# A list of units on one core: routing steps moved to the head of VectorE's list, and four smaller moves

## The chip, the core and the metric

The kernel runs on one core of a Trainium2 chip. Five engines work side by side on their own instruction lists: TensorE (PE, matrix products and transposes into PSUM), VectorE (DVE), ScalarE (ACT), GpSimd (POOL, which also issues the indirect transfers) and SyncE (SP, which issues the plain loads). An engine works through its list in order; an instruction that waits holds everything behind it on that engine. The metric is the device time of one execution in microseconds, taken as the median of several runs.

## What is computed

The reference is an mLSTM cell over 4 batches, 8 heads, 768 steps and a head width of 40, whose rows then go through a mixture of experts with top-1 routing in two levels (4 groups of 4 experts):

```python
m_new = max(f + m, i);  f_stab = exp(f + m - m_new);  i_stab = exp(i - m_new)
C = f_stab * C + i_stab * outer(v, k);   n = f_stab * n + i_stab * k
y = sigmoid(o) * (C @ q) / max(|n . q|, 1)          # x: 3072 rows of 320
g = argmax(x @ w_group);  e = argmax(x @ w_expert[g])  # one of 16 experts
out = softmax_g * softmax_e * (relu(x @ w1[g, e]) @ w2[g, e])
```

## The kernel before

The cell is computed in chunks of 128 steps: 6 chunks times 4 batches make 24 units, numbered u = 0 to 23, one after the other. The function `unit(u)` writes the instructions of one step of this pipeline, and since the schedule is manual there, each engine's list is in the order in which `unit` calls things. In unit u TensorE does, in this order: `scores(u)` (key times query, 16 products into `sp`), `turn(u - 2)` (three transposes of the finished rows `x` into the bank `av`, which ScalarE copies to `xT`), `state(u)` (update of the running sums `Cp`), a few transposes of the gate sums (`sum_on`), `back(u - 1)` (four transposes of the unit before into `av`, after ScalarE's copy of `xT` has freed that bank), `carried(u)` (the part of the result that comes from earlier chunks, into `avT`), in some units the routing products, and `values(u)` (the part from this chunk, into `avT`, which needs VectorE's masked scores `pt` and GpSimd's scaled values `vz`). VectorE does `masked` (two products, `pt`), `norm(u - 1)` and `rows(u - 1)` (`den` and `xn`). GpSimd does `rows2(u - 1)` (`x` from `xn` and `den`) and `vscale(u + 1)` (`vz`). ScalarE turns the gate, copies `Cp` to `Cs` (`state2`) and `avT` to `avs`.

Routing goes by groups of units, `GROUPS` = (0 to 3), (4 to 7), (8 to 11), (12 to 15), (16, 17), (18 to 21), (22, 23). After a group's rows are turned, `logits_of` makes its logits in the bank `lg`, and the generator `route` is appended to `chores`. Each `go_on(n)` runs its next n steps. The steps are: 1 maxima, differences (and an Exp on ScalarE); 2 `eq`; 3 `m2` and the one-hot rows of the levels; 4 `oh`; 5 the ranks, small products of `oh` on TensorE (L343 to L352); 6 and 7 slots and counts; 8 to 11 the weight of each row; 12 the slots are put on the list `ids`; 13 and 14 the running count. The tables `FIRST`, `RANKS`, `MID` and `END` say how many steps run at which place of which unit. An entry of `ids` is written by `put_id`, one indirect transfer by GpSimd (L448), one or two at the end of a unit and all that are left before unit 21. After the last of them SyncE reads the index list `ix` of the first expert, GpSimd gathers its rows `xg` (L543), and TensorE turns them in unit 23 (`turn_tasks`, into the banks `Cp`), ahead of `values(23)`. Expert 0 follows, then the others.

The weights of the first expert come during units 12 to 19. They are split into two parts by `split_tasks`: ScalarE casts a piece to fp32r (L607), and VectorE subtracts it from the original in the next unit (`lows`, L609). The gates' running maxima and sums are made by the generators `gate_sums`, of which `sum_on` runs a step or two in each unit; their transposes went into the free half of the bank `avT_125` (`AV[1]`).

Of the kernel before, what the change touches and what calls it, by code (L numbers as in the profile page):

```python
# [18 lines left out]
P = 128  # L19
B, H, S, D = 4, 8, 768, 40  # L20
NCH = S // P
NU = NCH * B
# [34 lines left out]
def bc(ap, shape):  # L57
    return ap.broadcast_to(list(shape))
# [3 lines left out]
def lstm_moe(ctx: ExitStack, tc: tile.TileContext, gates, qkT, nat, wcat, w1, w2, cst, seq, out):  # L62
    nc = tc.nc
# [56 lines left out]
    AV = [ps_a.tile([P, 512], F32, name=f"avT{i}") for i in range(2)]  # L120
# [5 lines left out]
    def busy(n):  # L126
        if n:
            t = ps_1.tile([P, 512], F32, name="busy", tag="lg")
        for _ in range(n):
            mm(t, ones_b, bc(ones_b.unsqueeze(1), (P, 4, P)), start=True, stop=True)  # L130
# [23 lines left out]
    def gate_o(u):  # L154
        o = st_[u]["nt"][:, 2 * DM:3 * DM]
        nc.scalar.activation(o, o, AF.Tanh, scale=0.5)
# [27 lines left out]
    def masked(u, r):  # L184
        t = st_[u]
        pt = wk.tile([P, 4, P], F32, name="pt", bufs=4)
        nc.vector.tensor_tensor(pt, t["pm"][r], bc(cs[:, C_UP:C_UP + P].unsqueeze(1), (P, 4, P)), op=ALU.mult)  # L187
        t["pm"][r] = pt
# [66 lines left out]

    def rows2(u):
        x = tail.tile([P, 3 * P], F32, name="x", bufs=NU - EUNITS)
        (nc.gpsimd if u < NU - 2 else nc.vector).tensor_tensor(  # L258
            x[:, 0:DM].rearrange("p (h d) -> p h d", d=D), st_[u]["xn"], bc(st_[u]["den"].unsqueeze(2), (P, H, D)), op=ALU.mult)
        st_[u]["x"] = x  # L260

# [22 lines left out]
    def bank_of(tag):  # L284
        return (pools["t"] if tag == "tp" else ps_1).tile([P, 512], F32, name=tag)
# [5 lines left out]
    def logits_of(u0, u1):  # L291

        n = u1 - u0
        bank = bank_of("lg")
        t = bank[:, P:2 * P]
        for k in range(3):
            for b in range(n):
                mm(t[32 * b:32 * b + 32, :], wc[:, k, :], st_[u0 + b]["xT"][:, k, :], start=(k == 0), stop=(k == 2))
        lT = wk.tile([P, P], F32, name="lT", bufs=1)
        nc.scalar.copy(lT[0:32 * n], t[0:32 * n])  # L300

        def back():
            nc.tensor.transpose(out=bank[:, 0:32 * n], in_=lT[0:32 * n], identity=ident[0:32 * n, 0:32 * n])
            chores.append(route(u0, u1, bank))

        backs.append(back)
# [91 lines left out]
    def go_on(n=1):  # L398
        for _ in range(n):
            if chores:  # L400
                with ExitStack() as st:
                    if not rt["manual"]:
                        st.enter_context(tc.high_priority())
                    if next(chores[0], StopIteration) is StopIteration:
                        chores.pop(0)
# [32 lines left out]
    def first_tokens():  # L438
        none, zero = rt["rows"]
        nc.sync.dma_start(itab[0:4 * P].rearrange("(p a) e w -> p (a e) w", p=P), none)  # L440
        nc.sync.dma_start(itab[NTOK], none[0:NE, 0, :])
        nc.sync.dma_start(x_d[0:1], zero[0:1])
# [338 lines left out]
    def run(stage, u):  # L781
        if 0 <= u < NU:
            stage(u)

    def do(tasks, n=99):
        while tasks and n:
            tasks.pop(0)()
            n -= 1

    def ix_of(r):  # L790
        return lambda i, m, w: ixs[r][0:m, i, w:w + 1]

    xgs, early_loads, early_splits = {}, [], []

    def unit(u):
        run(loads, u + 3)
        if u == 6:
            first_tokens()
        run(scores, u)
        go_on(FIRST.get(u, 0))  # L800
        run(lambda v: masked(v, 0), u)
        run(lambda v: masked(v, 1), u)
        run(turn, u - 2)
        if u == 0:
            busy(5)
        run(state, u)
        if u < 13:
            sum_on(SUMS.get(u, 1))
        run(back, u - 1)
        run(norm, u - 1)  # L810
        run(rows, u - 1)
        if u < B:
            run(rows2, u - 1)
        if u < NU - 2:
            run(vscale, u + 1)
        if u == NU - 3:
            run(vscale, u + 2)
        if u >= B:
            run(rows2, u - 1)
        do(lows)  # L820
        run(carried, u)
        go_on(RANKS.get(u, 0))
        if u % B == 1 and 1 < u < EUNITS:
            logits_of(u - 5, u - 1)
        if u == EUNITS + 1:
            logits_of(EUNITS - 2, EUNITS)
        if u == NU - 1:
            logits_of(EUNITS, NU - 2)
        if u == 11:
            go_on(2)  # L830
            chores.insert(0, first_experts())
        if u == EUNITS + 3:
            chores.append(early_counts())
        go_on(MID.get(u, 0))
        if u == NU - 1:
            do(rt["turns"])
        gate_o(u)
        run(state2, u)
        run(values, u)
        do(backs)  # L840
        go_on(END.get(u, 0))
        if u == 3:
            first_entries()
        if u == 5:
            first_rows()
        for _ in range(min(rt.get("old", 0), 1 if u < 16 else 2)):
            put_id()
        rt["old"] = len(ids)

    SUMS = {1: 2}  # L850
    FIRST = {19: 2, 20: 4}
    RANKS = {20: 1}
    MID = {6: 4, 7: 2, 8: 3, 9: 4, 10: 4, 11: 5, 12: 6, 13: 8, 14: 6, 15: 2, 16: 4, 17: 3, 18: 4, 19: 7, 20: 8, 21: 4, 22: 4}
    END = {6: 1, 10: 1, 14: 1, 18: 1}

    def gate_sums(lo, hi):
        fg, ig = G[:, 0, lo:hi], G[:, 1, lo:hi]
        q = nc.gpsimd if lo == 0 else nc.vector
        init = NEG if lo == 0 else M_[:, lo - 1:lo]
        nc.vector.tensor_tensor_scan(M_[:, lo:hi], fg, ig, init, op0=ALU.add, op1=ALU.max)  # L860
        l1 = max(lo, 1)
        q.tensor_tensor(Cg[:, lo:hi], ig, M_[:, lo:hi], op=ALU.subtract)
        yield
        nc.vector.tensor_tensor(Dl[:, l1:hi], G[:, 0, l1:hi], M_[:, l1 - 1:hi - 1], op=ALU.add)
        nc.vector.tensor_tensor(Dl[:, l1:hi], Dl[:, l1:hi], M_[:, l1:hi], op=ALU.subtract)
        yield
        nc.vector.tensor_tensor_scan(A_[:, lo:hi], Dl[:, lo:hi], low[:, lo:hi], 0.0 if lo == 0 else A_[:, lo - 1:lo],
                                     op0=ALU.add, op1=ALU.max)
        q.tensor_tensor(Cg[:, lo:hi], Cg[:, lo:hi], A_[:, lo:hi], op=ALU.subtract)
        yield  # L870
        cl, ch = lo // P, hi // P
        tp = AV[1][:, 2 * P:]
        n = ch - cl
        for i in range(n):
            s = slice((cl + i) * P, (cl + i + 1) * P)
            nc.tensor.transpose(out=tp[:, 32 * i:32 * i + 32], in_=Cg[:, s], identity=ident[0:32, 0:32])
            nc.tensor.transpose(out=tp[:, 32 * (n + i):32 * (n + i) + 32], in_=A_[:, s], identity=ident[0:32, 0:32])
        nc.scalar.activation(eb[:, cl:ch, :].rearrange("p c h -> p (c h)"), tp[:, 0:32 * n], AF.Exp)
        fl = floor[:, cl:ch, :].rearrange("p c h -> p (c h)")
        nc.scalar.activation(fl, tp[:, 32 * n:64 * n], AF.Exp, scale=-1.0)  # L880
        nc.vector.tensor_scalar(fl, fl, 2.0, None, op0=ALU.mult)
        if hi == S:
            yield
            over = post.tile([P, 1], BF16, name="over")[0:B * H]
            nc.vector.tensor_scalar(over, A_[:, S - 1:S], -RANGE, None, op0=ALU.is_le)
            yield
            tp = AV[1][:, 2 * P:]
            mm(tp[:, 0:1], ones_b[0:B * H], over, start=True, stop=True)
            nc.vector.tensor_scalar(wide, tp[:, 0:1], 1.0, None, op0=ALU.min)

# [2 lines left out]
    def sum_on(n=1):  # L893
        for _ in range(n):
            if sums and next(sums[0], StopIteration) is StopIteration:
                sums.pop(0)
# [49 lines left out]
    with tc.manual_schedule():  # L946
        for u in range(5, NU):
            if u == NU - 1:
                rt["turns"] = turn_tasks((0, 0), EARLY, xgs[0], Cp)
            if u == NU - 3:  # L950
                while ids:
                    put_id()
                load_ix(0)
            unit(u)
            do(early_loads, {12: 2, 13: 2, 15: 1, 16: 1, 17: 1, 18: 1, 20: 1, 21: 2, 22: 1, 23: 4}.get(u, 0))
            do(early_splits, {16: 1, 17: 1, 18: 1, 20: 1, 22: 1}.get(u, 0))
            if u == NU - 3:
                xgs[0] = load_x(EARLY, ix_of(0), True)
        go_on(4)
# [313 lines left out]
```

## Time and profile before

| | |
|---|---|
| median of 3 runs | 404.81 us (399.73 to 408.77) |
| the profiled execution | 399.82 us, span 398.2 us, mean granted TensorE clock 0.949 |
| busy | PE 366.3 us (92%), DVE 247.9 (62%), ACT 187.4 (47%), POOL 140.8 (35%) |
| transfers | 82.23 MB, mean 207 GB/s |

The span falls into two parts: the units, up to about 148 us, and the experts behind them. Busy shares are means over both, so each has to be read by itself. A number in square brackets behind a row of the time line is the time that the engine stood idle before it, and who ended that.

### The profile page before, as it was taken

What the parts mean: (1) busy time and instruction counts of PE and PEld (TensorE: products, weight loads), DVE (VectorE), ACT (ScalarE), POOL (GpSimd) and SP (SyncE); (2) the same over time, 40 slices, a digit from 0 to 9 for tenths busy, and PEclk for the clock granted to TensorE, in tenths of its full rate; (3) what the DMA queues carried; (4) which work ended last, traced back from release to release, by engine and by line L of the source; (5) the groups of instructions that cost most, each with busy time, mean ns of one, the idle gap of its engine ahead of it and who ended that gap; (6) DMA issues with size and microseconds to landing.
All of it is one profiled execution on the core that took longest, in us unless ns stands there. A gap on an engine that the chain in (4) does not pass through costs nothing.

```text
span 398.2 us, 9447 instructions
## 1 busy us (share of the span) xinstructions
PE 366.3 (92%) x3572; PEld 328.8 (83%) x3572; DVE 247.9 (62%) x636; ACT 187.4 (47%) x459; POOL 140.8 (35%) x199
## 2 busy tenths in 40 slices
PE   8898997979786698979999999999999999999993
PEld 3676775757665578979999999999999999999993
DVE  5767777856778267574799585576574725553520
ACT  2453434324533233264686555575574725545520
POOL 1264234526656504445223526315123313322210
PEclk9999999979979569987999999999999999999998
DMA  7878677586761620195608978586544567678500
GB/s 197 245 243 258 191 237 244 167 293 219 237 222 48 238 104 31 30 337 201 239 32 311 410 281 280 182 298 237 185 166 161 178 250 247 239 286 307 197 19 15
DMA packets 27383, 82.23 MB, mean 207 GB/s; under 512 B 8800, under 2 KB 12339, under 8 KB 23746
## 3 DMA queue, kind: packets, MB, share of 16 engines
q1 hardware_dynamic: 18946, 63.21, 46.8%
q0 software_dynamic: 4560, 13.16, 9.7%
q10 hardware_dynamic: 3824, 5.18, 3.8%
q8 instruction: 30, 0.49, 0.5%
q14 instruction: 23, 0.19, 0.2%
HBM read 72.70 MB, written 9.10 MB: 205 GB/s over the span
## 4 chain that ended last, share of the span: by engine, by line
PE 72%; DVE 11%; issue 8%; POOL 4%; ACT 3%; POOLq 1%; ACTq 0%; DVEq 0%
PE psh L714 14%; PE psh L682 7%; PE po L737 6%; PE po L738 6%; PE po L736 6%; PE sp L182 5%; PE avT L231 3%; PE av L239 3%; PE po L742 2%; PE av L264 2%; PE avT L222 2%; PE po L741 2%; POOL itab L448 2%; ACT xT L278 1%; PE tp L264 1%
## 5 line engine op out<-in xcount | busy, mean ns | idle before, releaser
L547 POOL DMA_INDIRECT out_dram<-y,ix x32 | 38.3, 1196 | 72.5 <-ACT y L748 57.7
L736 PE MATMUL po<-w2h,hh 128*128 128x320 f32 (+3 forms) x200 | 63.6, 318 | 0.0
L737 PE MATMUL po<-w2l,hh 128*128 128x320 f32 (+3 forms) x200 | 62.4, 312 | 0.0
L738 PE MATMUL po<-w2h,hh 128*128 128x320 f32 (+3 forms) x200 | 62.4, 312 | 0.0
L543 POOL DMA_INDIRECT xg<-x_d,ix x32 | 33.4, 1043 | 72.5 <-DMA ix<-itab 46.8
L609 DVE TENSOR_TENSOR w2l<-w2s,w2h 128x640 fp32r<-128x640 f32 x64 | 50.4, 817 | 12.0 <-ACT w2h L607 11.9
L671 DVE SCALAR_TENSOR_TENSOR hh<-psh,hh 128x240 fp32r<-128x240 f32 (+6 forms) x108 | 36.3, 366 | 21.0 <-ACT hh L668 20.6
L187 DVE TENSOR_TENSOR pt<-sp,cs 128x512 f32<-128x512 f32 x48 | 30.9, 684 | 22.0 <-PE sp L182 22.0
L668 ACT ACTIVATE hh<-psh 128x288 fp32r<-128x288 f32 (+8 forms) x68 | 30.2, 444 | 30.5 <-PE psh L714 15.9
L607 ACT CAST w2h<-w2s 128x640 fp32r<-128x640 f32 x64 | 43.2, 721 | 0.0
L682 PE MATMUL psh<-xhl,w1s 128*128 128x144 f32 (+3 forms) x336 | 41.3, 283 | 0.0
L682 PEld LDWEIGHTS psh<-xhl,w1s 128*128 128x128 f32 x336 | 40.9, 191 | 0.0
L258 POOL TENSOR_TENSOR x<-xn,den 128x320 f32<-128x320 f32 x22 | 18.8, 852 | 55.0 <-DVE xn L253 51.8
L714 PE MATMUL psh<-xhl,w1h 128*128 128x256 f32 (+5 forms) x224 | 37.1, 287 | 0.0
L736 PEld LDWEIGHTS po<-w2h,hh 128*128 128x128 f32 (+3 forms) x200 | 36.5, 183 | 0.0
L737 PEld LDWEIGHTS po<-w2l,hh 128*128 128x128 f32 (+3 forms) x200 | 36.5, 183 | 0.0
L738 PEld LDWEIGHTS po<-w2h,hh 128*128 128x128 f32 (+3 forms) x200 | 36.4, 182 | 0.0
L748 ACT ACTIVATE y<-po,ix 128x320 f32<-128x320 f32 (+3 forms) x24 | 12.7, 528 | 47.9 <-PE po L738 43.9
L448 POOL DMA_INDIRECT itab<-ent,slot x24 | 24.3, 1012 | 23.3 <-DVE ent L395 18.8
L714 PEld LDWEIGHTS psh<-xhl,w1h 128*128 128x128 f32 x224 | 31.2, 189 | 0.4 <-PE psh L714 0.2
L182 PE MATMUL sp<-qk 40*128 40x128 f32 x384 | 31.4, 303 | 0.0
L182 PEld LDWEIGHTS sp<-qk 40*128 40x128 f32 x384 | 26.2, 203 | 4.1 <-issue 3.0
(215 smaller groups left out, 717.8 us busy)
## 6 DMA issues: line engine op xcount, KB each, us to landing
w1s<-in_w_dram SPq DMA_DIRECT2D x13, 1536.0 KB
w2s<-in_w_dram SPq DMA_DIRECT2D x13, 1280.0 KB
nt<-in_nat_dram SPq DMA_DIRECT2D x24, 480.0 KB
qk<-in_qkT_dram SPq DMA_DIRECT2D x48, 160.0 KB
x_d<-x ACTq DMA_DIRECT2D x24, 192.0 KB
w1s<-in_w_dram SPq DMA_DIRECT2D x8, 384.0 KB
w2s<-in_w_dram SPq DMA_DIRECT2D x8, 320.0 KB
w1s<-in_w_dram POOLq DMA_DIRECT2D x1, 1536.0 KB, 10.1
```

Of the source, the lines that this page charges most:

```text
L182: mm(t["pm"][r][:, pr, :], qk[rs, 0, pr, :], qk[rs, 1, pr, :], start=True, stop=True)
L448: no_order("ids", nc.gpsimd.indirect_dma_start(out=itab_flat, out_offset=bass.IndirectOffsetOnAxis(ap=sl, axis=0), in_=tk, in_offset=None))
L543: return nc.gpsimd.indirect_dma_start(out=o, out_offset=None, in_=src, in_offset=bass.IndirectOffsetOnAxis(ap=idx, axis=0))
L547: return nc.gpsimd.indirect_dma_start(out=out, out_offset=bass.IndirectOffsetOnAxis(ap=idx, axis=0), in_=y, in_offset=None, bounds_check=N ...
L607: nc.scalar.copy(a, src[:, s])
L609: lows.append(lambda: nc.vector.tensor_tensor(o[rows], src[rows, s], a[rows].bitcast(F32), op=ALU.subtract))
L671: nc.vector.scalar_tensor_tensor(hh[:, f:f + per, dst], src[:, :, t], 0.0, hr.bitcast(F32)[:, :, t], op0=ALU.max, op1=ALU.subtract)
L682: ins = mm(ps[:, g * W:(g + 1) * W], w1s[:, s], xhl[:, k, :], start=(k == 0), stop=(k == 2))
L714: ins = mm(ps[:, g * W:(g + 1) * W], w[:, s], x, start=(n == 0), stop=(n == len(todo) - 1))
L736: mm(po[0:m], hh[:, f, t], w2h[:, s], start=st0, stop=False)
L737: mm(po[0:m], hh[:, f, t], w2l[:, s], start=False, stop=False)
L738: ins = mm(po[0:m], hh[:, f, tl], w2h[:, s], start=False, stop=sp0)
```

## The change

Five things move; the arithmetic is the same. First, the routing steps 1 to 4 of the groups that end with units 3, 7, 11 and 15 run at the head of units 6, 10, 14 and 18, in VectorE's list ahead of `masked`, and their rank products run in the middle of the unit instead of at its end. (The group (16, 17) stood like this already, in unit 20.) Later steps move to earlier units by a few places. Second, `carried(u)` goes from behind `back` to directly behind `turn`. Third, the cast of a weight piece goes from the end of the unit to a place ahead of `state2`, and so ahead of the copies of `avT`. Fourth, `rows2` of units 20 and 21 is done by VectorE instead of GpSimd. Fifth, the gate sums end one unit earlier and their transposes use the bank `lg`.

```diff
-        (nc.gpsimd if u < NU - 2 else nc.vector).tensor_tensor(
+        (nc.gpsimd if u < 20 else nc.vector).tensor_tensor(
...
         run(turn, u - 2)
...
+        run(carried, u)
         run(state, u)
-        if u < 13:
+        if u < 12:
             sum_on(SUMS.get(u, 1))
...
         do(lows)
-        run(carried, u)
         go_on(RANKS.get(u, 0))
...
-        if u == 11:
+        if u == 10:
             go_on(2)
             chores.insert(0, first_experts())
...
         gate_o(u)
+        do(early_splits, SPLITS.get(u, 0))
         run(state2, u)
         run(values, u)
         do(backs)
-        go_on(END.get(u, 0))
...
-    SUMS = {1: 2}
-    FIRST = {19: 2, 20: 4}
-    RANKS = {20: 1}
-    END = {6: 1, 10: 1, 14: 1, 18: 1}
+    SUMS = {1: 2, 4: 2}
+    FIRST = {6: 4, 10: 4, 14: 4, 18: 4, 20: 4}
+    RANKS = {6: 1, 10: 1, 14: 1, 18: 1, 20: 1}
+    SPLITS = {16: 1, 17: 1, 18: 1, 20: 1, 22: 1}
...
-        tp = AV[1][:, 2 * P:]
+        tp = bank_of("lg")
```

VectorE's list around unit 6, before (`pt` of unit 6 is the first row, `mx` to `oh` are steps 1 to 4 of the group (0 to 3)):

```order
L187 TENSOR_TENSOR pt<-sp,cs 128x512 x2
L881 TENSOR_SCALAR floor<-floor 128x64
L246 TENSOR_TENSOR den<-av,floor 128x8
L247 SCALAR_TENSOR_TENSOR den<-av,den 128x8
L248 RECIPROCAL den<-den 128x8
L253 SCALAR_TENSOR_TENSOR xn<-nt,av 128x320
L320 TENSOR_REDUCE mx<-lg 128x20
L322 TENSOR_TENSOR df<-lg,mx 128x80
L330 SCALAR_TENSOR_TENSOR eq<-df,cs 128x80
L333 TENSOR_REDUCE m_706<-eq 128x20
L334 TENSOR_TENSOR oh_702<-eq,m_706 128x80
L338 TENSOR_TENSOR oh<-oh_702 128x64
```

The same place after (`pt` is that of unit 6, `L860` and `L862` are a step of the gate sums):

```order
L320 TENSOR_REDUCE mx<-lg 128x20
L322 TENSOR_TENSOR df<-lg,mx 128x80
L330 SCALAR_TENSOR_TENSOR eq<-df,cs 128x80
L333 TENSOR_REDUCE m_666<-eq 128x20
L334 TENSOR_TENSOR oh_662<-eq,m_666 128x80
L338 TENSOR_TENSOR oh<-oh_662 128x64
L187 TENSOR_TENSOR pt<-sp,cs 128x512 x2
L860 SCALAR_TENSOR_TENSOR w1s<-w1s 32x256
L862 TENSOR_TENSOR w1s<-w1s 32x256
L246 TENSOR_TENSOR den<-av,floor 128x8
L247 SCALAR_TENSOR_TENSOR den<-av,den 128x8
L248 RECIPROCAL den<-den 128x8
```

The six routing instructions went from behind `xn` to a place ahead of the masks.

TensorE's list from unit 6's rank products on, before (`lg<-ohsum` is the last rank product, at the unit's end; then scores, turn, state, back and carried of unit 7, of whose eight rows two are shown):

```order
L347 MATMUL lg<-ohsum_85,ones_66 128x64
L182 MATMUL sp<-qk_103 128x128 x8
L264 MATMUL av<-cs,x 128x128 x3
L204 MATMUL Cp_123<-vz_105,nt 40x41 x8
L239 MATMUL av<-cs,avs 128x128 x4
L222 MATMUL avT_124<-qk_103,Cs 41x128
L222 MATMUL avT_125<-qk_103,Cs 41x128
```

The same place after (`avT<-pt,vz` is `values`, of unit 6 in the second and third row):

```order
L347 MATMUL lg<-ohsum_85,ones_66 128x64
L231 MATMUL avT_124<-pt,vz_104 41x128 x4
L231 MATMUL avT_125<-pt,vz_104 41x128 x4
L182 MATMUL sp<-qk_103 128x128 x8
L264 MATMUL av<-cs,x 128x128 x3
L222 MATMUL avT_124<-qk_103,Cs 41x128
L222 MATMUL avT_125<-qk_103,Cs 41x128
```

The ranks went ahead of `values(6)`, and `carried(7)` ahead of `state(7)` and `back(6)`.

GpSimd's list before, from the last write of `ids` ahead of the first expert's gather (`vz` of units 22 and 23, `x` of unit 20, the gathers, `x` of unit 21):

```order
L447 MEMSET sep 1x1
L448 DMA itab<-ent_72,slot 49168x4
L171 TENSOR_TENSOR vz_105<-nt,eb 128x8x40
L171 TENSOR_TENSOR vz_106<-nt,eb 128x8x40
L258 TENSOR_TENSOR x<-xn,den 128x320
L543 DMA xg<-x_d,ix 128x384 x2
L258 TENSOR_TENSOR x<-xn,den 128x320
```

After:

```order
L447 MEMSET sep 1x1
L448 DMA itab<-ent_72,slot 49168x4
L171 TENSOR_TENSOR vz_105<-nt,eb 128x8x40
L171 TENSOR_TENSOR vz_106<-nt,eb 128x8x40
L543 DMA xg<-x_d,ix 128x384 x2
```

Both `x` left GpSimd's list; each now stands in VectorE's directly behind its `xn`.

## Rows read from the trace of the kernel before

**Rows 1.** Busy time by stretch: PE, PEld, DVE, ACT, POOL, granted clock, DMA share.

```profile
40.55:44.93 4.38, 4.25 (x73) 3.29 (x72) 3.08 (x9) 1.56 (x5) 0.00 (x0) 1.00 0.43 145
34.32:101.36 67.04, 59.23 (x960) 45.79 (x959) 48.84 (x149) 27.20 (x96) 27.18 (x43) 0.95 0.74 231
84.03:91.25 7.22, 7.22 (x74) 5.53 (x72) 2.94 (x9) 1.61 (x5) 1.42 (x3) 0.53 0.72 234
101.62:121.30 19.68, 16.24 (x223) 12.54 (x221) 14.63 (x44) 7.60 (x24) 9.70 (x13) 0.83 0.65 210
125.79:145.82 20.03, 13.81 (x127) 10.04 (x125) 8.21 (x24) 4.22 (x12) 8.21 (x14) 0.57 0.48 166
186.00:370.00 184.00, 183.95 (x1367) 179.79 (x1365) 115.78 (x244) 106.11 (x215) 60.85 (x60) 1.00 0.66 239
```

**Rows 2.** Time line of TensorE: the rank products, one plain unit, two late waits.

```profile
40.30 0.19 PE L343 MATMUL lg<-oh,lt_b 128*128 128x64 bf16 x1 [1.37 <-DVE oh L338]
...
40.55 1.16 PE L182 MATMUL sp<-qk 40*128 40x128 f32 x16
41.65 0.55 PE L264 MATMUL av<-cs,x 128*128 128x128 f32 x3
...
43.92 1.07 PE L231 MATMUL avT<-pt,vz 128*41 128x128 f32 x16
...
61.04 0.19 PE L343 MATMUL lg<-oh,lt_b 128*128 128x64 bf16 x1 [1.69 <-DVE oh L338]
...
83.78 0.19 PE L343 MATMUL lg<-oh,lt_b 128*128 128x64 bf16 x1 [2.66 <-DVE oh L338]
...
132.04 0.90 PE L264 MATMUL av<-cs,x 128*128 128x128 f32 x3 [5.08 <-POOL x L258]
...
144.43 1.46 PE L264 MATMUL Cp<-cs,xg 128*128 128x128 f32 x6
```

**Rows 3.** What TensorE waited for, 0 to 150 us: sum, times, longest.

```profile
PE av L239 <- ACT xT L278: 3.4, 6, 1.1
PE avT L222 <- DVE wide L889: 0.7, 1, 0.7
```

**Rows 4.** Time line of VectorE: unit 6's masks, routing steps 1 to 4.

```profile
35.51 1.29 DVE L187 TENSOR_TENSOR pt<-sp,cs 128x512 f32<-128x512 f32 x2 [2.19 <-PE sp L182]
...
38.32 0.23 DVE L320 TENSOR_REDUCE mx<-lg 128x20 f32<-128x80 f32 x1
...
40.02 0.23 DVE L338 TENSOR_TENSOR oh<-oh 128x64 bf16<-128x64 f32 x1
```

**Rows 5.** Time line of GpSimd: `x` of unit 19, writes, `vz`, second gather.

```profile
121.38 0.72 POOL L258 TENSOR_TENSOR x<-xn,den 128x320 f32<-128x320 f32 x1 [2.21 <-DVE xn L253]
...
126.12 1.24 POOL L448 DMA_INDIRECT itab<-ent,slot  x1 [0.23 <-issue]
...
128.93 0.96 POOL L448 DMA_INDIRECT itab<-ent,slot  x1 [0.21 <-issue]
129.91 1.40 POOL L171 TENSOR_TENSOR vz<-nt,eb 128x320 f32<-128x320 f32 x2
...
135.19 0.95 POOL L543 DMA_INDIRECT xg<-x_d,ix  x1 [0.30 <-issue]
```

**Rows 6.** Time line of ScalarE in unit 16.

```profile
94.78 0.29 ACT L210 COPY Cs<-Cp 104x164 f32<-104x164 f32 x1 [0.91 <-PE avT L222]
95.30 0.81 ACT L233 COPY avs<-avT 128x256 f32<-128x256 f32 x2 [0.23 <-PE avT L231]
96.01 1.05 ACT L607 CAST w1h<-w1s 128x1024 fp32r<-128x1024 f32 x1
```

**Rows 7.** Time line of VectorE: a subtract of unit 21, `x` in unit 23.

```profile
125.70 0.82 DVE L609 TENSOR_TENSOR w2l<-w2s,w2h 128x640 fp32r<-128x640 f32 x1
...
143.15 0.49 DVE L258 TENSOR_TENSOR x<-xn,den 128x320 f32<-128x320 f32 x1
```

**Rows 8.** The two gathers `xg` of 133 to 140 us, issue to landing.

```profile
DMA to landing us min/median/max: 6.3/6.3/6.3
```

More of the change, by code (lines that the diff above doesn't have):

```diff
@@ L848, in unit @@
         rt["old"] = len(ids)
-    SUMS = {1: 2}
-    FIRST = {19: 2, 20: 4}
-    RANKS = {20: 1}
-    MID = {6: 4, 7: 2, 8: 3, 9: 4, 10: 4, 11: 5, 12: 6, 13: 8, 14: 6, 15: 2, 16: 4, 17: 3, 18: 4, 19: 7, 20: 8, 21: 4, 22: 4}
-    END = {6: 1, 10: 1, 14: 1, 18: 1}
+    SUMS = {1: 2, 4: 2}
+    FIRST = {6: 4, 10: 4, 14: 4, 18: 4, 20: 4}
+    RANKS = {6: 1, 10: 1, 14: 1, 18: 1, 20: 1}
+    MID = {6: 2, 7: 3, 8: 4, 10: 3, 11: 5, 12: 6, 13: 7, 14: 2, 15: 3, 16: 2, 17: 2, 18: 3, 19: 6, 20: 8, 21: 4, 22: 1}
+    SPLITS = {16: 1, 17: 1, 18: 1, 20: 1, 22: 1}
     def gate_sums(lo, hi):
@@ L886, in gate_sums @@
             yield
-            tp = AV[1][:, 2 * P:]
+            tp = bank_of("lg")
             mm(tp[:, 0:1], ones_b[0:B * H], over, start=True, stop=True)
@@ L955, in lstm_moe @@
             do(early_loads, {12: 2, 13: 2, 15: 1, 16: 1, 17: 1, 18: 1, 20: 1, 21: 2, 22: 1, 23: 4}.get(u, 0))
-            do(early_splits, {16: 1, 17: 1, 18: 1, 20: 1, 22: 1}.get(u, 0))
             if u == NU - 3:
```

## The prediction

> **What bounds the kernel now.** I read the busy time by stretch first, since the shares of the whole span mix two programs. Between 186 and 370 us TensorE is busy 183.95 of 184.00 us at full clock [rows 1]: the experts are bound by TensorE, nothing in them is touched, and whatever the units save moves that whole block forward and comes out at the end. So the question is only what the units cost, up to about 148 us.
>
> There a plain unit is bound by TensorE too: unit 7 takes 4.38 us with 4.25 busy and VectorE at 3.08 [rows 1]. But twelve units (6 to 17) take 67.04 us, where 12 times 4.38 is 52.6; the time line of TensorE shows where the rest goes [rows 2]. At the end of units 6, 10 and 14 the rank products wait 1.37, 1.69 and 2.66 us for the routing's `oh`, since VectorE does the routing steps last in the unit. After the 2.66 us the clock falls: unit 15 takes 7.22 us at a granted clock of 0.53 [rows 1], that is 2.84 us more than 4.38; after the shorter two it stayed at full. The same wait stands at the end of unit 18, with a slow unit behind it. In unit 22 TensorE waits 5.08 us for `x` of unit 20, which stands behind the writes of `ids` on GpSimd, and from there to 145.82 us the clock is 0.57 in the mean [rows 1, 2]. Besides, `back` waits 3.4 us in six places for the copy `xT`, and unit 12 0.7 us for `wide` [rows 3].
>
> **The change, part by part.**
>
> Routing steps at the head of the unit. Steps 1 to 4 last from 38.32 to 40.25, 1.93 us [rows 4]. VectorE stood idle 2.19 us ahead of unit 6's masks, so most of this falls into time that was empty; the logits are back in `lg` when scores begin. At worst the masks come 1.93 us later. TensorE has 2.27 us of work between the end of scores and `values` (41.65 to 43.92 [rows 2]), which hides that, so I put the new wait at 0 in units 6 and 10. Before unit 14, VectorE has about 1 us of its own list left over (unit 13 carries seven routing steps), so I leave 1.2 us of wait there, my estimate between 0 and 1.93. Gain: 1.37 + 1.69 + (2.66 - 1.2) = 4.5 us, and with a wait under the 1.69 that the clock survived, unit 15 keeps it: 2.84 more. Bounds: the masks' wait is 0 to 1.93 in each of the three.
>
> Gate sums in `lg`, one step earlier: the wait of 0.7 for `wide` goes, because `carried` no longer shares a bank with it. The second step in unit 4 makes a row late there and another in unit 7; I take 0.45 us against it (0 to one `x`, 0.72 [rows 5]).
>
> `carried` behind `turn`. It gives the copy of `xT` another 0.6 us before `back` needs the bank. Outside units 18 to 23, which are costed below, that leaves small change: the two short waits in units 16 and 17 and the 0.13 us between 4.25 busy and 4.38 in each plain unit [rows 1, 3]. I take 0.9 us for twelve units (0 to 2.2). Its price is that it now waits for ScalarE's copies of `avT` earlier: 1.65 us after `values` (scores and turn, 40.55 to 42.20 [rows 2]) instead of behind `back`. In the trace those copies end 0.5 to 0.6 us after `values`: hidden.
>
> Casts ahead of `state2`. A cast is 1.05 us; ScalarE idled 0.91 us before `state2` and 0.23 before the copies in unit 16 [rows 6], 1.14 together. The three casts of `w1` fit, just, so I cost them at 0; what they cost if that cover goes is the slower rival below.
>
> Units 6 to 17 together: 4.5 + 2.84 + 0.7 - 0.45 + 0.9 = 8.5 us.
>
> Units 18 to 20. Here VectorE becomes the bound. From 101.62 to 121.30, where `xn` of unit 19 ends, it was busy 14.63 of 19.68 us [rows 1]; the list is the same, reordered, and with some 0.9 us of waits left in it `xn` comes 4.1 us earlier. The wait in unit 18, the slow unit 19 and a wait for `xT` lie inside this and are not counted again. I expect TensorE to wait about 2 us for the masks in unit 20; it costs nothing beyond this.
>
> Units 21 to 23. With `x` of units 20 and 21 on VectorE (0.49 us each [rows 7]) the wait of 5.08 us goes. What is late next? First `vz` of unit 22, still behind the six writes: they end at 129.89 and it is there at 130.6 [rows 5]. Then the gathered rows: the second gather is issued at 135.19 and lands 6.3 us later, at 141.5 [rows 5, 8]. TensorE turned them at 144.43 [rows 2], so this chain (`xn` of unit 19, `x`, six writes, index list, gathers) had only 2.9 us of slack. Nothing in the change shortens it: it starts 4.1 us earlier with `xn`, and TensorE will stand before the turns for some 5 to 6 us. So of the 5.08 us and of the slow stretch behind it only 2.9 us come out.
>
> That new wait is as long as the one that goes, and the clock fell after that one. I charge a slow unit's price, 2.84 us, behind the turns; the bounds are 0 (it holds) and half of the 13.81 us that TensorE was busy at 0.57 [rows 1], 6.9.
>
> On the chain of writes a rule speaks against the fourth move. In the trace a write took 1.24 us, not 0.96, while VectorE did a subtract of 0.82 us [rows 5, 7]. The Trainium skill, page "GPSIMD Engine Reference", section "1. Specifications", says that GpSimd shares its SBUF interfaces with VectorE and contends with VectorE instructions that have two SBUF inputs; `x` on VectorE is such an instruction. By the rule its whole 0.49 us would be added to the chain, by the row 0.28/0.82 of it, 0.17; the sum would be 0.5 or 0.2 us less of a gain, and I leave both out.
>
> **Sum:** 8.5 + 4.1 + 2.9 - 2.84 = 12.7 us. The profiled execution took 399.82 us, so 387.1. It is the fast end of the runs: the median is 5.0 us above it, by which the sum would be 392. I forecast 388, nearer the profiled one, since waits of the kind that the change removes are a likely source of the spread.
>
> **The rivals.**
>
> The clock holds, or falls earlier and is back by the turns, and unit 14 does not wait: 12.7 + 2.84 + 1.2 = 16.7, 383 us. For it: the clock may fall during the long wait's idle time and recover on the turns. Against: it did not after the 5.08. Chance 0.12.
>
> The wait changes its place: the masks come later than TensorE's 2.27 us of cover in every routing unit, because VectorE enters the unit late. Then units 6, 10 and 14 wait 1.93 each (4.6 us less than I count) and unit 15 is slow again (2.84), and units 18 to 20 gain some 2 us less: 12.7 - 9.4 = 3.3, 396.5 us. For it: VectorE has 48.84 us of work in those 67.04, and less time will be left. Against: the 2.19 us idle ahead of unit 6's masks. Chance 0.13.
>
> The loads become the bound. In units 6 to 17 the DMA engines are busy 0.74 of 67.04 us [rows 1], 49.6 us; squeezed into 58.5 us that is 0.85. If they can do no more than 0.74, the 8.5 us are lost: 395.6 us. Against: SyncE's loads stand three units ahead. Chance 0.10.
>
> Slower: ScalarE's casts hold TensorE at `carried`. If ScalarE comes to a cast no earlier than the end of `values`, cast and copies take 1.05 + 0.81 = 1.86 us [rows 6], more than the 1.65 after which `carried` wants the bank, and `state` and `back` stand behind it on TensorE. That decides: once ScalarE has lost more than the 1.14 us of idle time, each of the five casts goes onto the path, with the copies queued behind it. The price is 4 to 5 us of casts and, if the clock falls each time, 5 times 2.84, together some 19 us against 12.7: 406 us. For it: the fit in unit 16 is 0.1 us. Against: a late copy shows up whole only where ScalarE was already late, and a wait of 0.2 us did not lower the clock anywhere in the trace. Chance 0.05.
>
> **How the numbers follow.** The forecast has 0.60. The low end takes in the first rival and 4 us of luck in the smaller bounds: 379. The high end is the sum on the median's basis, 392, with the masks waiting or the loads late: 399. About 2% (8 us) is what a measurement of this kernel can tell from no change; the line lies at 396.7. Of the second and third rival about half falls on each side of it: faster 0.60 + 0.12 + 0.10 = 0.82, taken as 0.80; slower 0.05; the rest 0.15.
>
> **What the profile after would show.** Right: no wait of TensorE for `oh` at the end of units 6, 10, 14 and 18; full clock from unit 6 to unit 19; unit 18's scores some 8 to 9 us earlier than 101.36; no wait for `x` in unit 22, a short one for `vz`, and a long one, 4 to 7 us, ahead of the turns of `xg`, with a low clock behind it. Wrong: `values` waiting for `pt` by 2 us in several units, `carried` waiting for `avs`, loads that hold `vz`, or turns that start without a wait (then something in units 21 to 23 took the time). The forecast fails by the most if the clock falls in units where I count on it.

## The result and the profile after

The changed kernel takes **384.04 us** (median of 4 runs, 382.14 to 384.81) against 405.35 us of the kernel before (4 runs beside it, 399.73 to 408.77): a ratio of 0.954 with a 95% interval of 0.942 to 0.966, so it is faster. Some executions of the kernel before run at a lower clock, and the ratio is formed from the fast executions of each kernel, so it is not 384.04/405.35. The forecast was 388.0 us with a range of 379 to 399.

The profiled execution took 384.81 us with a span of 383.2 us, against 399.82 and 398.2. All 15.0 us lie ahead of the experts: their first product starts at 133.00 us and not at 148.00. A table by stretch, with the starts of scores(6), of scores(18) and of the first expert product (`psh`) as its borders, shows where they came from:

| us | units 0 to 5 | units 6 to 17 | scores(18) to turns of `xg` | turns to first expert |
|---|---|---|---|---|
| before | 34.32 | 67.04 | 43.07 | 3.57 |
| after | 36.07 | 55.96 | 36.02 | 4.95 |
| saved | -1.75 | 11.08 | 7.05 | -1.38 |

The first view of the changed kernel is the busy time by stretch, with the columns of [rows 1]:

```profile
64.11:68.29 4.18, 4.18 (x73) 3.29 (x72) 3.30 (x12) 2.24 (x8) 2.49 (x4) 1.00 0.65 213
36.07:92.03 55.96, 54.54 (x956) 43.02 (x956) 45.69 (x146) 28.26 (x92) 26.59 (x43) 1.00 0.83 254
78.45:82.63 4.18, 4.18 (x73) 3.29 (x72) 2.84 (x10) 2.24 (x8) 2.51 (x4) 1.00 0.94 312
92.03:108.23 16.20, 13.51 (x224) 10.81 (x223) 14.37 (x47) 8.78 (x28) 10.60 (x14) 0.99 0.85 273
107.24:115.04 7.80, 7.80 (x74) 5.89 (x72) 5.33 (x24) 2.68 (x9) 5.73 (x11) 0.56 0.62 185
128.05:133.00 4.95, 4.64 (x30) 3.27 (x31) 1.84 (x5) 2.33 (x7) 0.00 (x0) 0.63 0.12 45
```

Units 6 to 17 now have TensorE busy for 54.54 of 55.96 us at full clock; before, it was 59.23 of 67.04 [rows 1]. A plain unit (64.11) has no gap left: 4.18 of 4.18, where 4.25 of 4.38 stood. Unit 15, 7.22 us at 0.53 before, takes 4.18 at full clock. From scores(18) to `xn` of unit 19 (92.03 to 108.23) VectorE is busy 14.37 of 16.20 us, so the list that bounds this part has little left in it. Behind unit 6 two slow stretches remain, at 107.24 and behind the turns.

The time line of TensorE of the changed kernel, at the places of [rows 2]:

```profile
17.03 0.55 PE L264 MATMUL av<-cs,x 128*128 128x128 f32 x3 [1.25 <-POOL x L258]
...
18.96 1.86 PE L231 MATMUL avT<-pt,vz 128*41 128x128 f32 x16
...
39.15 0.19 PE L343 MATMUL lg<-oh,lt_b 128*128 128x64 bf16 x1
...
58.46 0.19 PE L343 MATMUL lg<-oh,lt_b 128*128 128x64 bf16 x1
...
77.19 0.19 PE L343 MATMUL lg<-oh,lt_b 128*128 128x64 bf16 x1
...
106.49 0.66 PE L239 MATMUL av<-cs,avs 128*128 128x128 f32 x4 [2.04 <-ACT xT L278]
...
128.05 0.90 PE L264 MATMUL Cp<-cs,xg 128*128 128x128 f32 x3 [5.32 <-DMA xg<-x_d,ix]
129.16 0.90 PE L264 MATMUL Cp<-cs,xg 128*128 128x128 f32 x3 [0.20 <-DMA xg<-x_d,ix]
```

The rank products (L343) of units 6, 10 and 14 carry no wait. What is left is a wait for `x` in unit 2 with a slow product behind it, a wait for `xT` in unit 20, and one of 5.32 us for the gathered rows ahead of the turns, which took the place of the 5.08 us for `x` in unit 22 [rows 2].

The wait for `xT` is explained by ScalarE's time line there:

```profile
105.18 0.24 ACT L326 ACTIVATE ex<-df 128x40 f32<-128x40 f32 x1 [2.61 <-DVE df L322]
...
105.96 0.48 ACT L278 COPY xT<-av 128x384 f32<-128x384 f32 x1 [0.41 <-ACT x L270]
```

The routing's `Exp` (L326) stands ahead of the copy of `xT` in ScalarE's queue, as it did before the change, and VectorE delivers `df` late in this unit, so ScalarE idles 2.61 us with the copy behind it; before, it idled 0.95 us there and TensorE waited 1.06.

The chain to the gathers, on GpSimd (compare [rows 5]), and the time from issue to landing of the two gathers:

```profile
108.30 0.72 POOL L258 TENSOR_TENSOR x<-xn,den 128x320 f32<-128x320 f32 x1 [3.89 <-DVE xn L253]
...
109.21 1.00 POOL L448 DMA_INDIRECT itab<-ent,slot  x1
...
115.57 1.50 POOL L448 DMA_INDIRECT itab<-ent,slot  x1 [0.22 <-issue]
...
121.01 1.01 POOL L543 DMA_INDIRECT xg<-x_d,ix  x1 [2.51 <-DMA ix<-itab]
122.32 0.95 POOL L543 DMA_INDIRECT xg<-x_d,ix  x1 [0.30 <-issue]
```

```profile
DMA to landing us min/median/max: 6.8/6.9/7.0
```

The first gather of the kernel before, which [rows 5] leaves out:

```profile
133.88 1.01 POOL L543 DMA_INDIRECT xg<-x_d,ix  x1 [1.90 <-DMA ix<-itab]
```

It is the chain of before, `x` of unit 19, six writes, index list, two gathers, some 13 us earlier: `x` at 108.30 and not at 121.38, the second gather at 122.32 and not at 135.19 [rows 5].

### The profile page after: what moved, and what is told of

The parts are those of the page before. It is cut to its first block, busy times and chain, and to the rows that moved or that the text cites. A ratio compares the mean times of both kernels' runs of the same rounds, so it can differ in the third digit from the quotient of the medians.

```text
span 383.2 us, 9444 instructions
## 1 busy us (share of the span) xinstructions
PE 358.6 (94%) x3572; PEld 324.4 (85%) x3572; DVE 245.0 (64%) x638; ACT 189.4 (49%) x459; POOL 141.8 (37%) x197
## 4 chain that ended last, share of the span: by engine, by line
PE 42%; DMA 7%; issue 7%; DVE 3%; POOLq 1%; POOL 1%; SPq 1%; ACT 1%; ACTq 0%
PE psh L714 9%; PE psh L682 8%; PE po L738 5%; PE po L737 5%; PE po L736 5%; DMA ix<-itab 3%; DMA w1s<-in_w_dram 3%; PE po L742 2%; PE po L741 2%; PE tp L264 1%; PE lg L264 1%; PE psh L693 1%; DVE w2l L609 1%; PE psh L696 1%; POOLq L758 1%
## 5 line engine op out<-in xcount | busy, mean ns | idle before, releaser
L543 POOL DMA_INDIRECT xg<-x_d,ix x32 | 35.6, 1111 | 72.4 <-DMA ix<-itab 46.7
L748 ACT ACTIVATE y<-po,ix 128x320 f32<-128x320 f32 (+3 forms) x24 | 12.7, 529 | 47.0 <-PE po L738 43.0
L258 POOL TENSOR_TENSOR x<-xn,den 128x320 f32<-128x320 f32 x20 | 17.3, 865 | 44.4 <-DVE xn L253 39.5
L182 PE MATMUL sp<-qk 40*128 40x128 f32 x384 | 29.7, 297 | 0.0
L182 PEld LDWEIGHTS sp<-qk 40*128 40x128 f32 x384 | 25.0, 199 | 4.7 <-issue 2.9
```

What stands on the lines that cost most here:

```text
L182: mm(t["pm"][r][:, pr, :], qk[rs, 0, pr, :], qk[rs, 1, pr, :], start=True, stop=True)
L543: return nc.gpsimd.indirect_dma_start(out=o, out_offset=None, in_=src, in_offset=bass.IndirectOffsetOnAxis(ap=idx, axis=0))
```

## The experiments

Times are medians, with the kernel before measured beside each group. "Units 6 to 17" and "scores(18) to turns" are read from one profiled execution of each.

| kernel | us (lowest to highest) | before beside it | units 6 to 17 | scores(18) to turns |
|---|---|---|---|---|
| changed kernel | 384.04 (382.14 to 384.81) | 405.35 | 55.96 | 36.02 |
| changed kernel, again | 384.32 (382.81 to 388.66) | 401.21 | 55.84 | 36.33 |
| routing at the end | 405.17 (398.86 to 407.31) | 407.62 | 72.34 | 41.03 |
| `carried` behind the rows | 392.59 (386.07 to 396.79) | 404.38 | 58.56 | 41.78 |
| late `x` on GpSimd | 387.63 (386.09 to 388.60) | 404.38 | 57.15 | 38.43 |
| casts behind the unit | 385.71 (384.30 to 388.16) | 407.62 | 57.21 | 36.68 |
| `x` of 19 on VectorE | 386.28 (383.53 to 389.05) | 407.62 | 56.96 | 34.66 |
| routing one unit earlier | 386.15 (380.02 to 389.10) | 407.62 | 57.33 | 32.82 |
| the same, again | 382.56 (381.49 to 385.92) | 401.21 | 56.41 | 33.39 |
| both shorter | 383.09 (381.47 to 390.80) | 401.21 | 56.65 | 33.86 |
| waits filled | 382.04 (380.56 to 389.05) | 401.21 | 56.11 | 33.58 |
| `xg` wait filled whole | 384.00 (382.53 to 387.05) | 401.38 | 56.67 | 34.03 |

The changed kernel measured again has five of its six executions within 1.5 us of 384 and one at 388.66, so differences of 1 to 2 us between the lower rows can't be told.

**The routing steps back in their old order, the other four parts kept.** The last gate sum stands one unit later than in the changed kernel, since routing and sums share the bank `lg`; a first version without this ends in a deadlock and has no time.

```diff
-        if u < 12:
+        if u < 13:
...
+        go_on(END.get(u, 0))
...
-    SUMS = {1: 2, 4: 2}
-    FIRST = {6: 4, 10: 4, 14: 4, 18: 4, 20: 4}
...
+    SUMS = {1: 2, 4: 2, 11: 0}
+    FIRST = {19: 2, 20: 4}
...
+    END = {6: 1, 10: 1, 14: 1, 18: 1}
```

> The changed kernel with the tables of routing steps as they were (the last step of a group at the end of the unit), and the last gate sum one unit later, since the routing and the sums share the bank lg; the other parts stay. If the routing waits are the larger part of the gain: TensorE waits again for oh at the ends of units 6, 10, 14 and 18, by 1.4 to 2.7 us each, with a unit at about half the clock behind the longer ones; units 6 to 17 take 62 to 65 us and not 55.96, the time is 391 to 395 us. If the gain of these units came from carried behind turn: 384 to 386 us, units 6 to 17 within 1 us of 55.96.

Measured 405.17 us, next to 407.62 of the kernel before; the fastest executions are 398.86 and 397.68. Without this part nothing of the gain can be told from no change, and it is worse than either number expected. One row of the busy time by stretch, then the time line of TensorE; the profiled execution is one of 405.07 us:

```profile
34.47:106.81 72.34, 64.25 (x957) 49.57 (x956) 47.94 (x146) 27.07 (x92) 26.40 (x43) 0.86 0.69 216
```

```profile
40.81 0.19 PE L343 MATMUL lg<-oh,lt_b 128*128 128x64 bf16 x1 [2.09 <-DVE oh L338]
...
46.37 1.94 PE L231 MATMUL avT<-pt,vz 128*41 128x128 f32 x16
...
64.58 0.19 PE L343 MATMUL lg<-oh,lt_b 128*128 128x64 bf16 x1 [2.29 <-DVE oh L338]
...
89.32 0.21 PE L343 MATMUL lg<-oh,lt_b 128*128 128x64 bf16 x1 [3.35 <-DVE oh L338]
...
113.82 0.21 PE L343 MATMUL lg<-oh,lt_b 128*128 128x64 bf16 x1 [2.77 <-DVE oh L338]
```

All four waits are 0.6 to 0.7 us longer than in the kernel before (1.37, 1.69, 2.66 [rows 2], and 2.19 in unit 18). In units 6 and 10 TensorE comes to the rank products 0.36 us sooner behind the unit's scores, because four transposes of the gate sums, which stood in these units before, have moved out of them. `oh` comes 0.36 and 0.23 us later; in unit 6 VectorE now has a step of the gate sums ahead of the routing. First and last of the four transposes before, on TensorE, then the first row of that step here, on VectorE:

```profile
36.33 0.24 PE L876 MATMUL avT<-cs,w1s 32*128 32x32 f32 x1
...
36.53 0.22 PE L877 MATMUL avT<-cs,w2s 32*128 32x32 f32 x1
```

```profile
36.87 0.73 DVE L862 TENSOR_TENSOR_SCAN w1s<-w1s 32x256 f32<-32x256 f32 x1
```

So the longer waits are not the price of `carried` alone. Behind the 2.09 the value products take 1.94 us; the unit behind it and the one behind the 2.29 take 7.17 us each at a granted clock of 0.53, where behind the 1.37 and the 1.69 the clock had held. So units 6 to 17 come to 72.34 us in this execution, more than before the change.

**`carried` back behind `back` and the rows.**

```diff
-        run(carried, u)
         run(state, u)
...
         do(lows)
+        run(carried, u)
         go_on(RANKS.get(u, 0))
```

> The changed kernel with carried back behind back and the rows. If carried covers the copy of xT in each unit: a plain unit takes 4.38 us again and not 4.18, waits for xT stand in six places again, 1.5 us more, units 6 to 17 take 58.5 to 60 us, the time is 386.5 to 388.5 us. If the place of carried has no cost: 383.5 to 385 us.

Measured 392.59 us, beyond both; the fastest execution, 386.07, lies just below the first range. Units 6 to 17 are as the first theory has them. The second row is unit 12, with a wait of 0.42 us for `xT` in it, the third unit 8, without one:

```profile
34.57:93.13 58.56, 55.48 (x957) 42.87 (x956) 46.14 (x147) 27.79 (x92) 26.23 (x41) 1.00 0.79 247
63.22:67.89 4.67, 4.25 (x73) 3.29 (x72) 3.36 (x12) 2.15 (x8) 2.48 (x5) 1.00 0.79 221
44.12:48.50 4.38, 4.25 (x74) 3.29 (x72) 4.17 (x13) 2.14 (x8) 1.04 (x2) 1.00 0.87 199
```

The rest is in units 18 to 23: waits of `back` of 1.36, 2.10 and 2.04 us in units 18, 20 and 21, and 5.8 us more up to the turns than in the changed kernel. The parts are no sum. By the medians everything but `carried` keeps 11.8 of the 21.3 us, and everything but the routing 2.5, within the spread; by the fastest executions, each against the fastest of the kernel before beside it, it is 11.4 of 17.6 us, and -1.2.

**`x` of units 20 and 21 on GpSimd again.**

```diff
-        (nc.gpsimd if u < 20 else nc.vector).tensor_tensor(
+        (nc.gpsimd if u < NU - 2 else nc.vector).tensor_tensor(
```

> The changed kernel with x of units 20 and 21 on GpSimd again. If the chain of index writes and gathers sets when the turns of xg start, and the wait for x is only another place to stand: TensorE waits 4 to 5 us for x in unit 22 and at most 1.5 us for xg, the turns start within 2 us of 128.05, the time is 384 to 387 us. If the wait for x is a cost of its own: the wait for xg stays near 5 us as well, 389 us.

Measured 387.63 us, a ratio of 0.972 (0.962 to 0.983) against 0.954 (0.942 to 0.966) of the changed kernel; the intervals touch. TensorE, and below it GpSimd:

```profile
122.34 0.90 PE L264 MATMUL av<-cs,x 128*128 128x128 f32 x3 [1.82 <-POOL x L258]
...
130.15 0.87 PE L264 MATMUL Cp<-cs,xg 128*128 128x128 f32 x6
```

```profile
121.05 1.24 POOL L258 TENSOR_TENSOR x<-xn,den 128x320 f32<-128x320 f32 x1 [1.43 <-DVE xn L253]
122.44 1.01 POOL L543 DMA_INDIRECT xg<-x_d,ix  x1 [0.15 <-issue]
```

The wait for `xg` is gone and the turns start 2.1 us later than after the change, a little more than the 2 us expected: `x` itself now stands ahead of the gathers. The wait for `x` is 1.82 us and not 4 to 5, since in this execution the clock was 0.79 in the mean from scores(19) to scores(22) and TensorE came late. The time lies between the two ranges, nearer to the first, and the two waits exclude each other, as the theory of the chain has it.

**The casts of weights behind the unit, their old place.**

```diff
-        do(early_splits, SPLITS.get(u, 0))
         run(state2, u)
...
             do(early_loads, ...)
+            do(early_splits, SPLITS.get(u, 0))
```

> The changed kernel with ScalarE's weight casts at the end of the unit again, behind the copies of avT. If their place costs nothing because ScalarE has room in either: 383 to 385.5 us, no new wait of TensorE above 0.5 us in units 17 to 23. If a cast holds the next unit's copy of xT (1.05 us each, five of them, two seen by TensorE): waits for xT of about 1 us in units 17 to 21, 386 to 389 us.

Measured 385.71 us, a ratio of 0.965 (0.946 to 0.983). That is no difference that these runs can tell. TensorE waits for `xT` 1.5 us in unit 20, where the changed kernel waits 2.04, and 0.4 us in unit 23, and in no other unit from 17 on; no wait for a cast of 1.05 us is seen. The place of the casts brings nothing that shows.

**The gate sums in the bank of `AV` again.** 

> The changed kernel with the gate sums in the bank of AV and in their old steps. Units 0 to 5 took 1.75 us longer after the change (scores of unit 6 at 36.07 and not 34.32 us). If the shared bank lg causes that: scores of unit 6 at 34.3 to 34.8 us, a wait of about 0.7 us for wide in unit 12, the time 383 to 384 us. If the earlier carried or a late x causes it: scores of unit 6 near 36 us, the time 384.5 to 385.5 us.

Here `carried` stood ahead of sums that use its bank; the sums came out changed, most likely by that, and the kernel then ran another, longer program (567 us), so its time says nothing. The other profiles answer most of the question. `lg` holds the gate sums in every changed kernel of the table, and scores(6) start at 34.5 to 34.8 us in eight of the eleven further profiles. They start at 35.9 to 36.0 in the three that have, as the first one has, a wait of 1.2 us for `x` at 17.0 and a low clock behind it (0.60 to 0.66 from 17.1 to 21.3; 0.74 in the first). So most of the 1.75 us is not the bank's. The fifth part has a price all the same: in this run scores(6), which lie ahead of the longer program, start at 33.38 us.

```profile
7.48 1.16 PE L182 MATMUL sp<-qk 40*128 40x128 f32 x16
...
33.38 1.16 PE L182 MATMUL sp<-qk 40*128 40x128 f32 x16
```

That is 1.1 us ahead of the earliest of the eight: 0.4 us at the start, where the changed kernel's scores(0) stand at 7.90, behind a wait for the reader of `lg`, and 0.7 in unit 5, where it has the four transposes of the gate sums (0.36 us, out of unit 6) and a late `x`.

**`x` of unit 19 on VectorE.**

```diff
-        (nc.gpsimd if u < 20 else nc.vector).tensor_tensor(
+        (nc.gpsimd if u < 19 else nc.vector).tensor_tensor(
```

> The changed kernel with x of unit 19 on VectorE as well. If the chain xn of unit 19, x on GpSimd, six index writes, index list, gathers sets the turns of xg: four writes no longer stand behind xn (they can start at 104.5 us and not at 109.2), the last two follow the entries of units 16 and 17 at 110.3 us, the turns start 3 to 4 us earlier, the wait for xg falls from 5.3 to 1.5 or 2.3 us, the time is 380 to 381.5 us. If VectorE sets the end of these units, its 0.49 us more shows and nothing else: 384 to 385 us.

Measured 386.28 us, beyond both theories. The wait for `xg` did vanish, but because TensorE came late: units 20 and 21 took 14.30 us, 12.96 in the changed kernel (row of the busy time):

```profile
104.36:118.66 14.30, 10.30 (x120) 8.08 (x119) 11.41 (x41) 4.72 (x16) 10.20 (x16) 0.82 0.65 190
```

The last two writes still wait for the entries of units 16 and 17. The run doesn't tell the theories apart.

**The routing of units 12 to 15 finished one unit earlier**, so that four writes and not six stand behind `x` of unit 19.

```diff
-    MID = {..., 18: 3, 19: 6, ...}
+    MID = {..., 18: 8, 19: 1, ...}
```

> The changed kernel with the routing of units 12 to 15 finished in unit 18 (five steps more there, five fewer in unit 19), so that two index writes stand in unit 19 and four, not six, behind x of unit 19. If the chain of writes and gathers sets the turns of xg: they start 2 to 2.6 us earlier, the wait for xg is about 3 us, the time is 381 to 382.5 us. If VectorE is the bound up to there and the chain has slack: 383.5 to 385 us.

> The routing of units 12 to 15 finished in unit 18, once more, with more rounds. If the chain of writes and gathers sets the turns of xg when the clock holds: its fastest executions are 2 to 4 us below the fastest of the changed kernel. If the chain has slack in most executions, because low-clock units hold TensorE longer: medians within 1.5 us of each other.

The first time it took 386.15 us, above both numbers expected, with executions from 380.02 to 389.10; the fastest has the profile, and its turns start 32.82 us behind scores(18). In the second group 382.56 us beside 384.32 of the changed kernel (ratios to before 0.958, 0.953 to 0.964, and 0.961, 0.956 to 0.966); the fastest executions are 381.49 and 382.81. That is 1.3 to 1.8 us, between what the two theories gave, and within the intervals. The second profile, GpSimd and then TensorE:

```profile
106.10 0.73 POOL L258 TENSOR_TENSOR x<-xn,den 128x320 f32<-128x320 f32 x1
...
107.02 1.01 POOL L448 DMA_INDIRECT itab<-ent,slot  x1 [0.17 <-issue]
...
110.86 0.96 POOL L448 DMA_INDIRECT itab<-ent,slot  x1 [0.23 <-issue]
...
116.56 1.00 POOL L543 DMA_INDIRECT xg<-x_d,ix  x1 [2.66 <-DMA ix<-itab]
```

```profile
124.59 1.80 PE L264 MATMUL Cp<-cs,xg 128*128 128x128 f32 x6 [5.13 <-DMA xg<-x_d,ix]
126.32 1.94 PE L231 MATMUL avT<-pt,vz 128*41 128x128 f32 x16
```

From scores(18) to the turns it is 33.39 us and not 36.33 (the changed kernel in the same group): two writes fewer, 2.9 us sooner, and TensorE, which no longer waits 2.3 us for `xT` in unit 20, waits 5.13 us for `xg` again. So here the chain, not TensorE, sets the turns.

**Both shorter.** 

> The routing of units 12 to 15 finished in unit 18 and x of unit 19 on VectorE, together. If the chain still sets the turns behind the earlier routing: another 1 to 2 us below that kernel. If VectorE's own list up to unit 21 sets them by then: no difference, or 0.5 us more for the x it takes over.

383.09 us: nothing beyond the earlier routing. The last write ends 0.6 us sooner behind scores(18), but the index list is issued 3.6 us behind it, not 1.9: SyncE waits there for the writes to land, and no engine works on that.

**The waits filled.** To the earlier routing are added spare products that the transposes behind them overwrite.

```diff
+    WARM = {17: 3, 18: 3, 19: 3, 20: 6, "xg": 12}
+    def fill(t, n):
+        for _ in range(n):
+            mm(t, ones_b, bc(ones_b.unsqueeze(1), (P, 4, P)), start=True, stop=True)
```

> The kernel with the earlier routing, and spare bf16 products of 512 columns, each overwritten by the transposes behind it, ahead of the turns of units 17 to 20 (3, 3, 3 and 6 of them) and of xg (12), into the banks that these turns use. If idle TensorE time in these waits is what lowers the clock: the units 18 to 23 run at full clock, avT of value products takes 1.07 us in each and not 1.4 to 1.9, the times spread over less than 4 us and the median is 379 to 382 us. If the clock falls for another reason: the fillers only stand in the waits or cost up to 3 us, 385 to 389 us.

> The kernel with the filled waits, with 22 spare products ahead of the turns of xg and not 12 (0.22 us each at full clock, so 4.9 us). If idle time ahead of the turns is what lowers the clock behind them: the wait for xg falls from 2.63 to 0.6 us or less, the value products behind the turns take 1.07 to 1.15 us and not 1.57, the median is 380.5 to 382 us. If the chain of gathers comes early in many executions, the spare products stand in the way: 382.5 to 385 us.

The busy time of the first and, below it, of the second, up to the turns and behind them; then the stretch behind the turns in the second profile of the earlier routing (a wait of 5.13 us, no spare products) and in the kernel with the late `x` on GpSimd (no wait):

```profile
92.04:125.62 33.58, 30.62 (x424) 21.54 (x424) 27.73 (x90) 14.70 (x45) 21.63 (x32) 1.00 0.87 276
125.62:130.11 4.49, 4.25 (x30) 3.21 (x31) 2.19 (x7) 2.37 (x7) 0.00 (x0) 0.69 0.04 14
```

```profile
91.36:125.39 34.03, 32.78 (x434) 22.52 (x433) 28.10 (x90) 14.68 (x45) 21.63 (x32) 1.00 0.86 269
125.39:128.67 3.28, 3.20 (x30) 2.34 (x31) 1.84 (x5) 2.12 (x7) 0.00 (x0) 1.00 0.08 31
```

```profile
124.59:129.92 5.33, 5.33 (x30) 3.90 (x31) 2.19 (x7) 2.48 (x7) 0.00 (x0) 0.50 0.02 6
```

```profile
130.15:133.17 3.02, 3.02 (x34) 2.35 (x31) 2.92 (x8) 2.05 (x7) 0.00 (x0) 1.00 0.12 41
```

With 12 spare products ahead of the turns a wait of 2.63 us for `xg` is left and the stretch behind stands at 0.69; with 22 a wait of 0.51 us is left and it runs at full clock (3.28 us, where it was 4.95 after the change). Units 18 to 23 run at full clock too, but without spare products they stood at 0.99 in the second profile of the earlier routing, so there the products show nothing. The turns don't come sooner for it: the chain sets them. The first has the lowest median of all, 382.04 us, and five of its six executions lie between 380.6 and 382.7, one at 389.05, so they do not spread over less than 4 us as expected; its ratio of 0.955 (0.950 to 0.960) and the changed kernel's 0.961 (0.956 to 0.966) are not told apart. The second was to gain another 1 us and came out at 384.00. Its experts do start at 128.67 us, 1.44 ahead of the first's, and its last product stands at 373.08, 0.34 ahead, but its span ends 9.1 us behind that product and not 6.4. That tail is in one profile, and why it is longer stays open.

## Why the prediction came out right

The place of the gain and its kind were right, and the time, 4.0 us below the forecast, lies within the range. The forecast was set nearer to the fast end of the old kernel's executions, by a guess on their spread, and that came out: the median of before lies 5.5 us above its profiled execution, that of after 0.8 below. The account below covers the 15.0 us between the two profiled executions; the medians are 21.3 apart, and where the longer executions of before lose their time is not shown. By its own terms, on that basis (387.1 forecast, 384.8 measured):

*Units 6 to 17: 8.5 us forecast, 11.1 found.* The waits for `oh` went and unit 15 kept its clock. The routing's order carries this, as the first experiment shows. Two terms were too small. Unit 14 was charged a wait of 1.2 us for its masks and has none. And `carried` was put at 0.9 us; undoing it alone makes these units 2.6 us longer. The term took it for the cover of two short waits and 0.13 us a unit. But a plain unit became 0.20 us shorter (4.38 to 4.18), and of the two waits, which the prediction puts in units 16 and 17, the trace has one in unit 17 (0.45 us) and one in unit 18 (0.19). The wait for `xT` in units 6 to 17 did not shrink, one of 0.45 before and one of 0.53 after; with `carried` back and the other parts kept there are five, 1.8 us in all. Against that, `x` comes late in two units (0.35 and 0.54 us), twice the 0.45 charged. And 0.36 us of the 11.1 is no gain: the four transposes that moved from unit 6 to unit 5.

*Units 0 to 5: nothing forecast, 1.75 us lost.* The step that failed was to cost the early units at the second gate sum alone. 1.25 us of wait for `x` at 17.03 and a slow unit behind it are what this execution shows. The same kernel measured again waits 0.17 us there, and 1.00 for `vz` a unit earlier, and has 34.77 us. Eight of eleven further profiles do without the slow unit and start scores(6) 0.15 to 0.47 us later than before, so the rest, 1.3 to 1.6 us, differs between executions and is no fixed price of the change.

*Units 18 to the turns: 4.1 + 2.9 = 7.0 us forecast, 7.05 found.* That it fits so closely is luck: two misses of 0.4 us cancel. `xn` of unit 19 ends 3.7 us sooner behind scores(18), not 4.1, with VectorE bound as argued. Behind it 3.3 us came out, not 2.9. The prediction let the turns wait for the second gather; they start with the first (three transposes at 128.05, three more at 129.16), so the slack before was 4.2 us (133.88 + 6.3 against 144.43). Of this 0.9 went again, 0.7 because the gathers took 6.9 us to land and not 6.3.

The chain sets the turns in this execution: the wait of 5.32 us was announced as 5 to 6. The shorter chain moves the turns and the late `x` on GpSimd takes the wait back into unit 22, so this is shown. In the profiles with the casts behind the unit and with `x` of 19 on VectorE TensorE comes to the turns behind the rows, without a wait; there it sets them. Two details were off. TensorE waits in unit 20 for `xT`, behind ScalarE's `Exp`, not for the masks, though these are no sooner (the second ends at 107.26, `values` start at 107.24). And the short wait for `vz` in unit 22 did not come, because unit 21 was slow itself; the same kernel measured again, with unit 21 at 4.16 us, has it, 1.75 us.

On the writes, the price of VectorE's `x` was left out, as 0.17 us or 0.49. In the profile after, `x` (115.01 to 115.50) lies beside the write at 114.30 for 0.25 us, and that write takes its usual 0.96, which is one row only; the one that grows, to 1.50, lies beside the subtract `w2l` (115.42 to 116.24), as the long ones do in three other profiles (1.31 to 1.55). The Trainium skill, page "GPSIMD Engine Reference", section "1. Specifications", has GpSimd contend with VectorE instructions of two SBUF inputs; both are such instructions, and the trace agrees for `w2l`, with 0.35 to 0.59 us, and shows nothing for `x`.

*The clock behind the turns: 2.84 us forecast, 1.38 found against before.* The clock did fall, as the low end of the busy rows shows, and it goes with the wait: behind waits of 5.1 to 5.6 us, in four profiles, this stretch takes 4.87 to 5.61 us at 0.50 to 0.63, and in three without a wait 3.02 to 3.04 at 1.00 (a fourth, where the clock was low ahead of the turns already, has 3.36 at 0.89). With the wait filled it is 3.28, so 4.95 us is 1.7 to 1.9 over full clock; a whole unit's price was too much for a piece of a unit.

Together 12.7 - 1.75 + 2.6 + 0.05 + 1.45 = 15.0 us, the difference of the spans.

*The rivals.* Masks that come too late did not show: `values` waits for `pt` nowhere in units 6 to 17. The loads are no bound: the DMA engines are busy 0.83 of units 6 to 17, and 0.94 in unit 15, without a wait. ScalarE's casts hold nothing, in either place. The rival of a clock that holds came half true, in unit 14.

## What to carry to other kernels

A wait at the end of a pipeline stage is paid twice where it lets the clock fall, so a step on a second engine is worth moving to where that engine was idle, and the other moves are worth little until that wait is gone: without the routing part the four others gave nothing that could be told. Before a wait is counted as gained, follow the chain that ends next, with all its transfers, and take its slack as the gain; that found the wait of 5 us for `xg` here, and the sum of 7.0 us held (7.05) with two misses of 0.4 us that cancelled. What a wait costs in clock is to be sized by the work that stands behind it, and it differs between executions of the same kernel.

## What was not expected of the hardware

A low clock followed the same wait in one execution and not in another. In the changed kernel and in the one with `carried` behind the rows, TensorE waits for `x` at 17.03 us, 1.25 and 1.26 us, with the same products at the same times ahead of it from 7.9 us on (the two lists are alike up to there); the value products behind it take 1.86 us in the first (time line above) and 1.07 in the second:

```profile
17.03 0.55 PE L264 MATMUL av<-cs,x 128*128 128x128 f32 x3 [1.26 <-POOL x L258]
...
18.97 1.07 PE L231 MATMUL avT<-pt,vz 128*41 128x128 f32 x16
```

The Trainium skill, page "TensorE: Matmul & The Clock Gate", section "What's actually happening", says that the moment at which the clock changes differs between runs of one kernel; it says so of a kernel's start, and here two kernels that are alike up to the place show it at 19 us.

Such falls in some executions and not in others are the likely source of the spread, 380.0 to 390.8 us among the kernels that keep both the routing and `carried` moved; that is an inference from one profile of each.

With 22 spare bf16 products in the wait ahead of the turns the clock stood at full behind them, where behind bare waits of 5.1 to 5.6 us it stood at 0.50 to 0.63.

In the changed kernel `x` on GpSimd took 0.72 us at 108.30 and 1.76 us at 101.51, when VectorE did the fp32r subtract of a weight. GpSimd, then VectorE:

```profile
101.51 1.76 POOL L258 TENSOR_TENSOR x<-xn,den 128x320 f32<-128x320 f32 x1
```

```profile
101.47 1.22 DVE L609 TENSOR_TENSOR wsk<-w1s,wsk 64x1024 fp32r<-64x1024 f32 x1
```
